# A constant tile of 41 words instead of 1, and one of 41 instead of 17, in a fused attention and SoLU kernel

## The chip, the cores and the metric

The kernel runs on one core of a Trainium2 chip. What counts is the time of one execution on the device in microseconds; shown is the median of three runs. One further execution was recorded by the hardware profiler, and every row below is from that one.

## What is computed

Sliding-window attention with a few "sink" keys (4 batches, 8 heads, 768 positions, head size 64) is followed, token by token, by two dense layers with a SoLU and a layer norm between them:

```python
scores = scale * np.matmul(q, k.transpose(0, 1, 3, 2))
keep = is_sink | in_window          # n_sink = 4, window = 128
a = softmax(np.where(keep, scores, -1e9))
x = np.matmul(a, v)                 # 3072 tokens x 512
h = x @ w_in                        # 512 -> 1024
solu = h * softmax(h)
ln = (solu - mu) / np.sqrt(var + 1e-06) * g_ln
out = ln @ w_out                    # 1024 -> 512
```

The weights arrive as 64-bit floats.

## The kernel before

**Tiles of work.** The 3072 tokens are cut into 24 blocks of 128. A block goes through scores, softmax, product with the values, the first layer (`hidden`, line 748), the SoLU, and the second layer (`project`, line 839). The order in which all these steps are issued, for all blocks together, is a table of numbers (`ORDER`) written into the kernel; each engine does its instructions in that order, and all loads and stores are issued on the queue of SyncE (SP).

**The two layers on TensorE.** Both use 4-byte words of the type float32r and give float32 accuracy by splitting: a matrix is the sum of a high and a low part, and a product is three matmuls, high x high, high x low and low x high. In `hidden` the stationary operand (the one that a weight load puts into the array) is a 128x128 slice of `xh` or `xl`, and the moving operand is 512 columns of `w1h` or `w1l`. There are 4 slices, 2 halves of the 1024 outputs and 3 products, so 24 matmuls for a block and 576 in all:

```python
for m, (a, w) in enumerate(((xh, w1h), (xh, w1l), (xl, w1h))):
    nc.tensor.matmul(st["h", n][:, cols], a[:, kt, :], w[:, kt, cols], ...)
```

`project` has the same form with `uh`, `ul` (stationary) and `w2h`, `w2l` (moving, 512 columns): 8 slices of 3 products, 24 matmuls for a block. Only the last block does its 512 columns as two halves of 256, so there are 552 matmuls of 512 columns and 48 of 256. Each matmul has its own weight load of 128 columns, which the engine makes while the matmul before it is still streaming.

**Weights.** 16 blocks of raw weights (`wraw`, 512 KB each, 4096 bytes in each of 128 partitions) are loaded by `fetch_w` (line 374) near the start. ScalarE and VectorE take them apart into `w1h`, `w1l` (in the pool `consts`) and `w2h`, `w2l` (in `wpool`, in the very buffers that `wraw` has given back).

**Where tiles lie.** Within a partition the pools lie one behind the other, and each tile is given its length rounded up to a multiple of 32 bytes. So the length of an early tile sets the place of all that is allocated behind it. `consts` holds `val`, `w1h`, `w1l`, `ok`, `allok` and, as its last tile, `general`, one word that says whether the inputs need the other, general path of the kernel. `wpool` follows, then `cpool` with the identity matrices `ident` and `ident_r`, masks, and `neg_half` (a word that holds -0.5), then `keys`, and then `sb` with `xh`, `xl`, `uh`, `ul` and all that passes through a block. In the built program the places are (bytes, and what is left modulo 256):

| tile | before | mod 256 | after | mod 256 |
|---|---|---|---|---|
| w1h, w1l (moving, layer 1) | 16544, 32928 | 160 | the same | 160 |
| w2h, w2l (moving, layer 2), wraw | 49408 + 4096 i | 0 | 49568 + 4096 i | 160 |
| ident, ident_r | 82176, 82688 | 0 | 82336, 82848 | 160 |
| keys | 85536 | 32 | 85792 | 32 |
| uh (stationary, layer 2) | 106912 + 2048 i | 160 | 107168 + 2048 i | 160 |
| xl (stationary, layer 1) | 121504 + 2048 i | 160 | 121760 + 2048 i | 160 |
| ul (stationary, layer 2) | 150176 + 2048 i | 160 | 150432 + 2048 i | 160 |
| xh (stationary, layer 1) | 181408 + 2048 i | 160 | 181664 + 2048 i | 160 |

The slices that single matmuls take begin at multiples of 512 bytes (stationary) and 2048 bytes (moving) within these, or 1024 in the halves of the last block, which leaves the remainder by 256 as it is.

Of the kernel before, what the change touches and what calls it, by code (L numbers as in the profile page):

```python
# [9 lines left out]
F32 = mybir.dt.float32  # L10
F32R = mybir.dt.float32r
I32 = mybir.dt.int32
# [111 lines left out]
P = 128  # L124
# [13 lines left out]
def kernel(  # L138
# [23 lines left out]
    with ExitStack() as fast:  # L162
        general = _banded(fast, tc, q, k, v, n_sink, window, w_in, w_out, g_ln, out, val, wts, wpool, consts)
# [7 lines left out]
def _outside(nc, consts, n_f, w_f):  # L171

    ok = consts.tile([P, 4], F32, name="ok")
    nc.vector.tensor_scalar(ok[:, 0:1], n_f, 0.0, None, op0=ALU.is_ge)
    nc.vector.tensor_scalar(ok[:, 1:2], n_f, float(NSK), None, op0=ALU.is_le)
    nc.vector.tensor_scalar(ok[:, 2:3], w_f, 1.0, None, op0=ALU.is_ge)
    nc.vector.tensor_scalar(ok[:, 3:4], w_f, float(P), None, op0=ALU.is_le)
    allok = consts.tile([P, 1], F32, name="allok")
    nc.vector.tensor_reduce(allok, ok, axis=AX.X, op=ALU.min)
    general = consts.tile([P, 1], I32, name="general")  # L180
    nc.vector.tensor_scalar(general, allok, -1.0, 1.0, op0=ALU.mult, op1=ALU.add)
    return general


def _banded(ctx, tc, q, k, v, n_sink, window, w_in, w_out, g_ln, out, val, wts, wpool, consts):
# [13 lines left out]
    cpool = ctx.enter_context(tc.tile_pool(name="cpool", bufs=1))  # L199
# [28 lines left out]
    def outside(_, j):  # L228
        st["general"] = _outside(nc, consts, n_f, w_f)
# [120 lines left out]
        for i in range(2):  # L350
            nc.vector.tensor_scalar(of_lows[:, i, :], by_head, lows[:, i:i + 1], None, op0=ALU.mult)

    neg_half = cpool.tile([P, 17], F32, name="neg_half")[:, 0:1]
    nc.vector.memset(neg_half, -0.5)


# [707 lines left out]
```

## Time and profile before

| | |
|---|---|
| median of 3 runs | 407.3 us (406.33 to 408.24) |
| the profiled execution | 407.82 us, its span 406.1 us |
| TensorE (PE) busy | 389.2 us, 96% of the span |
| VectorE, ScalarE, GpSimd busy | 301.4, 254.0, 158.2 us |
| moved by DMA | 76.24 MB, 188 GB/s on the mean |

The span is that of the core's instructions; the 1.7 us between it and the execution's own time lie outside them. A matmul's record runs past the start of the next one, since matmuls are pipelined: its duration says little of what it costs, and what counts is the distance from one start to the next.

### The profile page before, as it was taken

To read this page: it belongs to the slowest core of one execution; us is meant where nothing else is said; L and a number is where in the kernel's file an instruction comes from. 1 tells how busy PE (TensorE), PEld (TensorE's weight loads), DVE (VectorE), ACT (ScalarE), POOL (GpSimd) and SP (SyncE) were. 2 spreads that over 40 slices of the span, in tenths; PEclk is the share of its full clock that TensorE was granted. 3 is DMA by queue.
4 is the path that set the end of the run, shared out by engine and by line. 5 is a ranking of instruction groups with operands and counts; after the bars stand their busy time and mean duration, and the time that the engine had idled before them with its cause. 6 is when DMAs were issued, how large, how long until landed. Compare 5 with 4: busy or idle time off the path is not lost.

```text
span 406.1 us, 10168 instructions
## 1 busy us (share of the span) xinstructions
PE 389.2 (96%) x3667; PEld 309.4 (76%) x3667; DVE 301.4 (74%) x883; ACT 254.0 (63%) x698; POOL 158.2 (39%) x312
## 2 busy tenths in 40 slices
PE   3798999999999999999999999999999999999996
PEld 2465768877877878787778888878888788878885
DVE  3989999999999999789979687783763745542340
ACT  3999999857677687656637746655454553342451
POOL 6713171615756463713533341562520552400100
PEclk9999999999999999999999999999999999999999
DMA  7999569999998878999886667959275635503011
GB/s 208 339 301 255 137 141 209 180 222 240 240 231 232 249 214 220 268 210 277 206 224 172 161 212 149 246 167 257 103 196 149 185 126 156 178 4 106 26 53 59
DMA packets 86573, 76.24 MB, mean 188 GB/s; under 512 B 45868, under 2 KB 75444, under 8 KB 86516
## 3 DMA queue, kind: packets, MB, share of 16 engines
q1 hardware_dynamic: 86516, 75.52, 71.8%
q8 instruction: 31, 0.51, 0.5%
q14 instruction: 26, 0.21, 0.2%
HBM read 48.76 MB, written 26.87 MB: 186 GB/s over the span
## 4 chain that ended last, share of the span: by engine, by line
PE 71%; DMA 10%; DVE 7%; ACT 5%; POOL 3%; issue 2%; SPq 2%; POOLq 0%; ACTq 0%; DVEq 0%
PE o L839 28%; PE h L748 26%; PE av L728 8%; PE banks L567 5%; ACT sc L606 2%; DMA ub<-ud 2%; DMA kn<-in_k_dram 1%; DMA qn<-in_q_dram 1%; DVE sc L597 1%; DMA wraw<-in_moe_w_in_dram 1%; DMA ud<-u 1%; DMA vn<-in_v_dram 1%; PE av L718 1%; DMA pb<-pd 1%; PE banks L665 1%
## 5 line engine op out<-in xcount | busy, mean ns | idle before, releaser
L606 ACT ACTIVATE sc<-sc,nmx 128x132 f32<-128x132 f32 x192 | 75.6, 398 | 15.2 <-DVE nmx L597 15.2
L839 PE MATMUL o<-w2h,uh 128*128 128x512 f32 (+1 forms) x200 | 78.6, 393 | 0.0
L748 PE MATMUL h<-w1h,xh 128*128 128x512 f32 x192 | 77.5, 404 | 0.4 <-DVE u L763 0.4
L839 PE MATMUL o<-w2h,ul 128*128 128x512 f32 (+1 forms) x200 | 77.5, 388 | 0.0
L839 PE MATMUL o<-w2l,uh 128*128 128x512 f32 (+1 forms) x200 | 77.2, 386 | 0.0
L748 PE MATMUL h<-w1l,xh 128*128 128x512 f32 x192 | 75.3, 392 | 0.0
L748 PE MATMUL h<-w1h,xl 128*128 128x512 f32 x192 | 75.2, 392 | 0.0
L626 POOL TENSOR_TENSOR pn<-sc,rs 128x512 f32<-128x512 f32 x38 | 39.2, 1045 | 42.6 <-DMA pb<-pd 17.5
L758 ACT ACTIVATE e<-h,nm 128x1024 f32<-128x1024 f32 x24 | 26.8, 1117 | 39.3 <-DVE nm L753 37.1
L679 POOL TENSOR_SCALAR_AFFINE_SELECT pc<-pt 128x512 f32<-128x512 f32 x40 | 28.1, 711 | 57.0 <-DVE pt L656 38.9
L597 DVE CUSTOM_DVE_ANT_0 sc<-banks,bias 128x132 f32<-128x132 f32 x192 | 46.8, 286 | 2.4 <-PE banks L567 0.7
L748 PEld LDWEIGHTS h<-w1h,xh 128*128 128x128 f32 x192 | 36.0, 188 | 11.6 <-issue 2.3
L839 PEld LDWEIGHTS o<-w2h,uh 128*128 128x128 f32 x200 | 37.6, 188 | 9.6 <-issue 1.5
L839 PEld LDWEIGHTS o<-w2h,ul 128*128 128x128 f32 x200 | 37.6, 188 | 8.4
L839 PEld LDWEIGHTS o<-w2l,uh 128*128 128x128 f32 x200 | 37.6, 188 | 7.8
L753 DVE TENSOR_REDUCE nm<-h 128x1 f32<-128x1024 f32 x24 | 29.2, 1218 | 18.8 <-PE h L748 18.6
L748 PEld LDWEIGHTS h<-w1h,xl 128*128 128x128 f32 x192 | 36.0, 188 | 8.4 <-DVE xl L737 0.5
L825 DVE TENSOR_TENSOR ul<-ur,uh 128x512 fp32r<-128x512 f32 x40 | 29.1, 739 | 16.6 <-ACT uh L821 15.9
L748 PEld LDWEIGHTS h<-w1l,xh 128*128 128x128 f32 x192 | 36.1, 188 | 6.8
L567 PE MATMUL banks<-keys,q 32*64 32x200 f32 (+3 forms) x1280 | 36.8, 331 | 2.6 <-ACT keys L548 1.5
L606 ACT ACTIVATION_READ_ACCUMULATOR sc<-sc,nmx 128x1 f32 x192 | 36.8, 192 | 0.0
L567 PEld LDWEIGHTS banks<-keys,q 32*64 32x64 f32 (+1 forms) x1280 | 27.7, 133 | 10.3 <-issue 5.2
(142 smaller groups left out, 702.3 us busy)
## 6 DMA issues: line engine op xcount, KB each, us to landing
ud<-u SPq DMA_DIRECT2D x20, 512.0 KB, 3.3
ub<-ud SPq DMA_DIRECT2D x80, 128.0 KB, 3.8
pb<-pd SPq DMA_DIRECT2D x76, 128.0 KB, 3.8
vn<-in_v_dram SPq DMA_DIRECT2D x24, 256.0 KB, 5.1
out_dram<-ob SPq DMA_DIRECT2D x23, 256.0 KB, 3.3
kn<-in_k_dram SPq DMA_DIRECT2D x12, 384.0 KB, 5.8
qn<-in_q_dram SPq DMA_DIRECT2D x12, 384.0 KB, 8.7
pd<-pn SPq DMA_DIRECT2D x34, 128.0 KB, 3.7
```

Source lines behind the costliest of these rows:

```text
L567: nc.tensor.matmul(st["s", n, g][ROWS[y], x, 256 * j + at:256 * j + at + wide], st["q", n][rows, m, ROWS[y]], kk[rows, m].rearrange("p b x ...
L597: nc.vector.tensor_tensor_reduce(out=st["sc", n][:, h], in0=st["s", n, g][:, x, 256 * j + BLK:256 * j + BLK + SEG], in1=bias0 if c == 0 el ...
L606: nc.scalar.activation(sc[:, h], sc[:, h], AF.Exp, bias=nmx[:, h:h + 1], scale=-1.0, accum_out=ssum[:, h:h + 1])
L626: nc.gpsimd.tensor_tensor(st["pn", n][:, 2 * i:2 * i + 2].rearrange("p b h x -> p h b x"), st["sc", n][:, :, PARTS[i]].rearrange("p h (b x ...
L665: nc.tensor.matmul(t[ROWS[i ^ 1 if old and y == 0 else i], y, h], st["pn", n][ROWS[y], h, ROWS[i]], ident[ROWS[y], ROWS[y]], start=True, s ...
L679: nc.gpsimd.affine_select(st["pc", n][:, hs], st["pt", n][:, hs], pattern=[[0, HB], [1, P]], compare_op=ALU.is_ge, fill=0.0, base=0, chann ...
L728: nc.tensor.matmul(acc[ROWS[x], r, :], vals[:, 2 * r + x, :], p[:, 2 * r + x, :], start=alone, stop=alone or (r, i) == (NPAIR - 1, 1))
L748: nc.tensor.matmul(st["h", n][:, cols], a[:, kt, :], w[:, kt, cols], start=(kt == 0 and m == 0), stop=(kt == KT1 - 1 and m == 2))
L753: nc.vector.tensor_reduce(nm, st["h", n], axis=AX.X, op=ALU.max, negate=True)
L758: nc.scalar.activation(e, st["h", n], AF.Exp, bias=st["nm", n], scale=1.0, accum_out=se)
L825: nc.vector.tensor_tensor(ul, turned_u(n, g4), st["uh", n, g4].bitcast(F32), op=ALU.subtract)
L839: nc.tensor.matmul(st["o", n, i], a[:, kt % 4, :], part(w, kt)[:, i * wide:(i + 1) * wide], start=(kt == 0 and m == 0), stop=(kt == KT2 - ...
```

## The change

`general` becomes the first column of a tile of 41 words instead of a tile of 1: its room goes from 32 to 192 bytes. `neg_half` becomes the first column of 41 words instead of 17: its room goes from 96 to 192 bytes. What lies between the two moves up by 160 bytes, what lies behind both by 256. No instruction is added, removed or put elsewhere: on all five engines the rows of the two programs are the same, in the same order, and differ in addresses alone.

```diff
@@ -177,7 +177,7 @@
     nc.vector.tensor_reduce(allok, ok, axis=AX.X, op=ALU.min)
-    general = consts.tile([P, 1], I32, name="general")
+    general = consts.tile([P, 41], I32, name="general")[:, 0:1]
     nc.vector.tensor_scalar(general, allok, -1.0, 1.0, op0=ALU.mult, op1=ALU.add)
     return general
@@ -350,7 +350,7 @@
-    neg_half = cpool.tile([P, 17], F32, name="neg_half")[:, 0:1]
+    neg_half = cpool.tile([P, 41], F32, name="neg_half")[:, 0:1]
     nc.vector.memset(neg_half, -0.5)
```

## Rows read from the trace of the kernel before

**Rows 1.** The page: busy time, share of the span and instructions of TensorE.

```profile
PE 389.2 (96%) x3667; PEld 309.4 (76%) x3667; DVE 301.4 (74%) x883; ACT 254.0 (63%) x698; POOL 158.2 (39%) x312
```

**Rows 2.** The page: the chain that ended last, by engine.

```profile
PE 71%; DMA 10%; DVE 7%; ACT 5%; POOL 3%; issue 2%; SPq 2%; POOLq 0%; ACTq 0%; DVEq 0%
```

**Rows 3.** Waits of TensorE: total, times, longest, the two largest.

```profile
PE spread L266 <- DVE lows L347: 5.3, 1, 5.3
PE banks L567 <- ACT early_keys L548: 1.7, 1, 1.7
```

**Rows 4.** Timeline of TensorE, 274 to 277 us: start, duration, line.

```profile
274.33 0.39 PE L748 MATMUL h<-w1l,xh 128*128 128x512 f32 x1
...
275.24 0.39 PE L748 MATMUL h<-w1h,xl 128*128 128x512 f32 x1
...
275.92 0.39 PE L748 MATMUL h<-w1h,xl 128*128 128x512 f32 x1
276.15 0.40 PE L839 MATMUL o<-w2h,uh 128*128 128x512 f32 x1
```

**Rows 5.** The same timeline, 277.8 to 279.7 us.

```profile
277.79 0.39 PE L839 MATMUL o<-w2l,uh 128*128 128x512 f32 x1
...
279.66 0.39 PE L839 MATMUL o<-w2h,uh 128*128 128x512 f32 x1
```

**Rows 6.** The chain in order of time, 262 to 326 us: start, us, what.

```profile
270.77 5.54 PE h L748 x24
276.31 5.61 PE o L839 x24
281.92 4.80 PE h L748 x21
...
312.30 4.91 PE o L839 x21
```

**Rows 7.** Stretches, line 839 alone: length, PE busy (count), clock, DMA.

```profile
60.00:120.00 60.00, 11.88 (x48) 8.82 (x48) 1.00 1.01 220
120.00:228.00 108.00, 35.67 (x144) 26.73 (x144) 1.00 0.86 219
228.00:260.00 32.00, 11.67 (x48) 8.94 (x48) 1.00 0.80 200
260.00:406.10 146.10, 83.66 (x360) 63.80 (x360) 1.00 0.45 131
```

**Rows 8.** The chain in order of time, 225 to 262 us.

```profile
225.68 2.95 PE h L748 x12
...
228.70 0.56 SPq L486
...
259.58 2.51 PE av L728 x41
```

**Rows 9.** Stretches, line 748 alone.

```profile
120.00:228.00 108.00, 44.46 (x178) 32.83 (x179) 1.00 0.86 219
...
260.00:406.10 146.10, 47.74 (x192) 35.66 (x192) 1.00 0.45 131
```

**Rows 10.** Timeline of TensorE, last block: matmuls of 256 columns.

```profile
396.19 0.28 PE L839 MATMUL o<-w2h,uh 128*128 128x256 f32 x1
...
396.90 0.28 PE L839 MATMUL o<-w2h,uh 128*128 128x256 f32 x1
```

**Rows 11.** DMA issues: count, KB each, median us to landing.

```profile
ud<-u SPq DMA_DIRECT2D x20, 512.0 KB, 3.3
...
wraw<-in_moe_w_in_dram SPq DMA_DIRECT2D x8, 512.0 KB, 5.5
wraw<-in_moe_w_out_dram SPq DMA_DIRECT2D x8, 512.0 KB, 5.7
```

**Rows 12.** Stretch 10 to 20 us: PE, PEld, DVE, ACT, POOL busy, clock, DMA share, GB/s.

```profile
10.00:20.00 10.00, 6.99 (x71) 5.10 (x63) 9.27 (x42) 9.07 (x31) 7.41 (x19) 1.00 1.08 337
```

**Rows 13.** Groups of TensorE: busy us, mean ns, idle before.

```profile
L814 PE MATMUL banks<-ident,ud 128*128 128x128 f32 x32 | 4.4, 274 | 0.0
```

## The prediction

> **What bounds the kernel now.** I read the page first for the engine that is never idle. It is TensorE, busy for 96% of the span [rows 1], and 71% of the chain that ended last is its work [rows 2]. Then its waits, to see whether it is held up by anyone: the longest is 5.3 us at the very start, the next 1.7 us [rows 3]. So from about 60 us on TensorE is fed without a break, and the time is the sum of the distances between its matmuls. All stretches that I cite have a granted clock of 1.00, the level of 2.4 GHz [rows 7, 9, 12], so the clock explains no difference between them.
>
> The last view is the one that this change is about: the distance from one matmul's start to the next, in the two layers, which do the same thing (128x128 stationary, 512 moving columns, float32r, a new weight load for each). In layer 1 the starts go from 274.33 to 275.92 us in 7 steps (5 matmuls between the rows are left out, beside the one shown), 1.59 / 7 = 227 ns [rows 4]. In layer 2, some 3 us later, they go from 277.79 to 279.66 us in 8 steps, 1.87 / 8 = 234 ns [rows 5]. The chain says the same of whole runs: 24 of layer 2 take 5.61 us (234 ns each) and 21 take 4.91 (234); 24 of layer 1 take 5.54 (231) and 21 take 4.80 (229), where each run of layer 1 begins with a few slower ones before it settles at 227 [rows 6]. I find the same two levels up to the end of the trace. At its settled pace, then, a matmul of layer 2 costs 234 - 227 = 7 ns (6.6 before rounding: 233.75 - 227.1) more than the same matmul of layer 1.
>
> **What the change does to them.** What can differ between equal matmuls is where their operands lie. In layer 1 the moving and the stationary operands both begin at 160 modulo 256; in layer 2 the moving begin at 0 and the stationary at 160. The start of the slow pace is also where the place changes: up to 276.15 us the words that move are `w1`, from there on `w2`, and the weight load for the first `uh` still went on under the last `w1` matmul, which kept its 227 ns [rows 4]. After the change layer 2 stands as layer 1 does, both operands at 160, and I expect it to take layer 1's pace. The rest of the program is the same rows on every engine.
>
> - *Layer 2, 512 columns.* Its 552 such matmuls lie as follows: 48 from 60 to 120 us, 144 from 120 to 228, 48 from 228 to 260, and 360 behind that, less the 48 of 256 columns, 312 [rows 7]. I count 144 + 312 = 456. The 48 of 228 to 260 us I leave out: in that stretch a chain that begins with layer 1 on TensorE at 225.68 goes through SyncE's queue and loads and comes back to TensorE at 259.58 [rows 8], so that what TensorE saves inside it turns into a wait at its end. The chain hangs on TensorE's own work at its start, so what was saved before 228 us is kept. The 48 before 120 us I leave out for the same reason (TensorE is not on the chain in most of that time). 456 x 6.6 ns = 3.0 us.
> - *Layer 2, the 48 of 256 columns.* From 396.19 to 396.90 us 6 steps take 0.71 us, 118 ns each [rows 10]. No row shows such a matmul with operands that agree. Bounds: nothing, or the same 6.6 ns each, 0.3 us. I take nothing, since 118 is close to half of 234 but no farther above half of 227 than the reading allows.
> - *Layer 1.* Its places modulo 256 stay. Where its runs follow layer 2 directly, the slower matmuls at their start should go: a run of 21 at 4.80 us holds 4.80 - 21 x 0.2271 = 0.03 us of that [rows 6], with one such change for each of the 24 blocks a gain of 0.7 us at the most. On the other side runs that settle only after a few matmuls keep layer 2 from its full gain, by about as much. I set the one against the other.
> - *The raw weights.* `wraw` moves with `w2`, so 16 loads of 512 KB now land at 160 instead of 0. They take 5.5 to 5.7 us to landing; the stores of `u`, which leave SBUF from places at 160 and are as large, take 3.3 [rows 11], and no load here lands 4096-byte rows at 160. So nothing for sure; I take nothing, being nearest to that store, which bears its start at 160 without harm. Upper bound: 8.4 MB at the 337 GB/s of the second 10 us are 25 us of transfers [rows 12]; if each row of 4096 bytes cost one more piece of 256, that is 1/16 or 1.6 us, and all of it on the path only if nothing else covered it. VectorE and ScalarE, busy 9.3 and 9.1 of those 10 us [rows 12], cover most of it.
> - *Identity matrices, masks.* They are read by short transposes and mask operations, whose pace no pair of rows compares. The transposes of `u` by `ident`, at both ends of the run, are 32 [rows 13]; at 6.6 ns either way that is 0.2 us. I take nothing.
>
> The Trainium skill, in "DMA: Bandwidth & Descriptors", section "How a descriptor splits into AXI transactions", says that a transaction must start at a multiple of 256 B, so that a descriptor which doesn't is cut into one more. By that the loads of `wraw` would each have 17 transactions for 16, and the kernel could lose up to the 1.6 us above; no run here shows it so far.
>
> **The sum.** 407.82 us of the profiled execution less 3.0 is 404.8. That execution was 0.5 us above the median of the runs (407.3), so for the median I forecast 407.3 - 3.0 = 404.3 us, or 0.74% less. A difference under 0.5% (2.0 us) is about what a measurement of this kernel can't tell from none.
>
> **The rivals.**
> *No change.* Where the operands lie may have nothing to do with the 7 ns; the layers also write to different PSUM tiles, and take their stationary operand from different producers. Then the time stays 407.3. For it speaks only that a difference between two groups is not an experiment; against it that both paces are so steady, and that neither DMA nor another engine changes at 276.15 us. The Trainium skill is on its side: "SBUF — State Buffer", section "Who interferes with whom", gives TensorE two independent read ports, one for the moving operand and one for weight loads, and says that only the port pair of VectorE and GpSimd contends; by that rule the two operands can't hinder each other wherever they lie. The trace at least has some cause that this rule doesn't name, since 227 and 234 ns stand side by side.
> *Slower: the true period is 512 bytes.* The stationary tiles of both layers move by 256, `w1` doesn't. Modulo 512 `w1` lies at 160, and `xh`, `xl` lie at 160 before and at 416 after, so layer 1 would lose the agreement that it has, and fall to 234 ns. That costs 370 matmuls of layer 1 in the two stretches that count [rows 9] 6.6 ns each, 2.4 us, with more before 120 us. Layer 2 would agree only in its products with `ul` (both at 416), a third of 456: 1.0 us back at best, nothing if one disagreeing product spoils the next. The time is 408.7 to 409.7. Against it: the last `w1` matmul before 276.15 us runs while a `uh` slice at 416 modulo 512 is loaded (it lies at 111008), and the 4 steps from 275.24 to 276.15 take 0.91 us, 227.5 ns each [rows 4]. It decides if agreement is judged modulo 512 or more in most matmuls, not in one at a boundary.
> *Faster, but not by as much.* If the chain of 228 to 260 us [rows 8] or loads elsewhere don't move up with TensorE, the 144 matmuls before it give nothing: 312 x 6.6 = 2.1 us, 405.2. With half of the bound on `wraw` as well, 406.
>
> **How the numbers follow.** The forecast's case, layer 2 at layer 1's pace and most of it kept, 403.5 to 405.2: 60%. Faster by less than that (405.2 to 406.5): 13%. No effect: 17%. Slower by the period of 512 bytes, or by `wraw` without the gain: 7%. More than forecast (all 552 and the 48 short ones, and layer 1's starts, 4.6 us in all): 3%. The range is to leave out the slower case and part of "no effect" on its upper side, with the runs' own spread, and reaches to 407.5; below, to 402.8 for the largest gain. The likeliest case alone has 403.0 to 405.2. Of the 13% half are under 0.5%. So faster 0.69, same 0.23, slower 0.08.
>
> **What would show it.** Right: the distance of starts at line 839 is 227 ns in settled runs, as at line 748 before, and stays there across the change of layer; line 748 stays at 227; the page has the same instructions, and TensorE's waits stay small but for some tenths near 100 and 260 us. Wrong: line 839 stays at 234 (places don't matter); line 748 goes to 234 (period 512); line 839 is faster, but TensorE waits more, and the waits name DMA, SyncE or GpSimd; or `wraw` lands later than 5.5 us and the first 60 us grow.

## The result and the profile after

The changed kernel takes 404.51 us (median of seven runs) against 407.31 us of the kernel before. One of the seven took 974.09 us and is left out of the ratio; the other six took 402.86 to 404.88. The ratio is 0.9915, 95% interval 0.9895 to 0.9935, so it is 0.85% faster, 3.5 us by the ratio, where 3.0 were forecast. The page of the kernel after, its first line and the chain by engine:

```profile
PE 384.6 (96%) x3667; PEld 308.6 (77%) x3667; DVE 301.2 (75%) x883; ACT 254.1 (63%) x698; POOL 158.6 (39%) x312
PE 82%; DMA 5%; DVE 5%; ACT 3%; issue 2%; SPq 2%; POOL 1%; DVEq 0%; ACTq 0%; POOLq 0%
```

The instructions are the same in number, TensorE is busy for the same share of the span [rows 1], and more of the chain is its own [rows 2]. The timeline of TensorE after, at the change from layer 1 to layer 2 that rows 4 and 5 show (start, duration, line):

```profile
271.38 0.39 PE L748 MATMUL h<-w1l,xh 128*128 128x512 f32 x1
...
273.65 0.39 PE L748 MATMUL h<-w1h,xl 128*128 128x512 f32 x1
273.87 0.39 PE L839 MATMUL o<-w2h,uh 128*128 128x512 f32 x1
274.10 0.39 PE L839 MATMUL o<-w2l,uh 128*128 128x512 f32 x1
...
276.37 0.39 PE L839 MATMUL o<-w2h,ul 128*128 128x512 f32 x1
```

Ten steps of layer 1 (271.38 to 273.65) take 2.27 us, 227 ns each, as before [rows 4]. Ten steps of layer 2 (274.10 to 276.37) take 2.27 us as well, 227 ns each, where they took 234 [rows 5]; the pace doesn't change where the layer changes. The chain of the kernel after, in order of time, with the pieces that answer to rows 6 and 8 (start, us, what):

```profile
224.21 2.95 PE h L748 x12
...
256.40 3.65 PE av L728 x64
260.05 5.66 PE o L839 x24
...
268.48 5.55 PE h L748 x24
274.04 5.44 PE o L839 x24
279.48 4.76 PE h L748 x21
```

A run of 24 of layer 2 went from 5.61 to 5.44 us (226.7 ns each). The run of 21 of layer 1 behind it went from 4.80 to 4.76 [rows 6]: it doesn't begin with slower matmuls any more. TensorE's waits, the two longest, are 5.0 and 1.9 us, both in the first 60 us (compare [rows 3]):

```profile
PE spread L266 <- DVE lows L347: 5.0, 1, 5.0
PE banks L514 <- DVE nmx L597: 1.9, 1, 1.9
```

### The profile page after: what moved, and what is told of

Its sections match the earlier page's. It is cut to its first block, busy times and chain, and to the rows that moved or that the text cites. A ratio compares the mean times of both kernels' runs of the same rounds, so it can differ in the third digit from the quotient of the medians.

```text
span 401.6 us, 10168 instructions
## 1 busy us (share of the span) xinstructions
PE 384.6 (96%) x3667; PEld 308.6 (77%) x3667; DVE 301.2 (75%) x883; ACT 254.1 (63%) x698; POOL 158.6 (39%) x312
## 4 chain that ended last, share of the span: by engine, by line
PE 82%; DMA 5%; DVE 5%; ACT 3%; issue 2%; SPq 2%; POOL 1%; DVEq 0%; ACTq 0%; POOLq 0%
PE o L839 31%; PE h L748 29%; PE av L728 9%; PE banks L567 6%; DMA wraw<-in_moe_w_in_dram 2%; DMA kn<-in_k_dram 2%; DMA pb<-pd 2%; PE ws L408 2%; ACT sc L606 1%; PE banks L665 1%; PE av L718 1%; DVE sc L597 1%; PE banks L814 1%; DVE keys L540 1%; PE banks L514 1%
## 5 line engine op out<-in xcount | busy, mean ns | idle before, releaser
L839 PE MATMUL o<-w2h,uh 128*128 128x512 f32 (+1 forms) x200 | 77.7, 389 | 0.0
L839 PE MATMUL o<-w2h,ul 128*128 128x512 f32 (+1 forms) x200 | 76.3, 381 | 0.0
L839 PE MATMUL o<-w2l,uh 128*128 128x512 f32 (+1 forms) x200 | 76.2, 381 | 0.0
L825 DVE TENSOR_TENSOR ul<-ur,uh 128x512 fp32r<-128x512 f32 x40 | 28.1, 715 | 16.9 <-ACT uh L821 16.9
L763 DVE SCALAR_TENSOR_TENSOR u<-h,e 128x1024 f32<-128x1024 f32 x24 | 29.2, 1219 | 8.8 <-ACT e L758 8.5
```

Of the source, the lines that this page charges most:

```text
L763: nc.vector.scalar_tensor_tensor(u, st["h", n], -1.0 / DFF, st["e", n], op0=ALU.mult, op1=ALU.mult, accum_out=nmu)
L825: nc.vector.tensor_tensor(ul, turned_u(n, g4), st["uh", n, g4].bitcast(F32), op=ALU.subtract)
L839: nc.tensor.matmul(st["o", n, i], a[:, kt % 4, :], part(w, kt)[:, i * wide:(i + 1) * wide], start=(kt == 0 and m == 0), stop=(kt == KT2 - ...
```

## The experiments

The main theory, called A below, is that the moving words and the stationary words of a matmul must begin at the same place modulo 256 bytes. All ten kernels issue the same instructions in the same order as the kernel before, and differ in where tiles begin. The distance d is the place of the moving words less that of the stationary ones, modulo 256: before, 0 in layer 1 and 96 in layer 2. In each kernel the same three pieces of the chain near 270 us are read, a run of 24 of layer 1, one of 24 of layer 2 and one of 21 of layer 1, since nothing but the matmuls themselves bounds them.

**The two edits apart, and all at another place.** Three kernels, timed six to twelve times each.

The first keeps only `general` (d = 96 in both layers):

```diff
-    general = consts.tile([P, 1], I32, name="general")
+    general = consts.tile([P, 41], I32, name="general")[:, 0:1]
```

Expected: 

> Only the longer tile of general: w1 stays at 160, w2 moves to 160, and the stationary tiles of both layers to 64 modulo 256. Theory A (moving and stationary words must begin at the same place modulo 256): both layers disagree now, settled distances of 234 ns at line 839 and at line 748; layer 1 loses 2.5 to 3.5 us, so the ratio to the kernel before is 1.005 to 1.010. Theory B (only the place of the moving words counts, 160 is good, 0 is bad): 227 ns in both layers, ratio 0.990 to 0.994, as with the whole change. Theory C (places do nothing, the gain was something else in the program's layout): line 748 at 227, line 839 at 234, ratio 0.997 to 1.003.

Ratio 1.0049, interval 1.0032 to 1.0065 (409.13 us). The chain of this kernel:

```profile
271.97 5.67 PE h L748 x24
277.64 5.60 PE o L839 x24
283.24 4.90 PE h L748 x21
```

Now layer 1 is slow too: 4.90 us for 21, 233 ns each, and layer 2 stays so (5.60 us for 24, 233 ns). One half of the change alone makes the kernel slower, with `w2` at the very place that it has in the whole change. That rules out theory B (160 is a good place for moving words) and theory C. The loss, 2.0 us by the ratio, is smaller than the 2.5 to 3.5 that were expected, and the ratio just under the expected 1.005 to 1.010. Layer 1's runs were not all settled at 227 before: the run of 21 lost 4.90 - 4.80 us [rows 6], 5 ns for each matmul and not 7.

The second keeps only `neg_half` (d = 160 in layer 1, 0 in layer 2):

```diff
-    neg_half = cpool.tile([P, 17], F32, name="neg_half")[:, 0:1]
+    neg_half = cpool.tile([P, 41], F32, name="neg_half")[:, 0:1]
```

Expected: 

> Only the longer tile of neg_half: w1 stays at 160, w2 stays at 0, the stationary tiles of both layers move to 0 modulo 256. Theory A (agreement modulo 256): the layers change roles, 227 ns at line 839 and 234 at line 748; the gain of one is the loss of the other, ratio 0.997 to 1.003. Theory B (the moving words' place alone): as before, 234 at line 839 and 227 at line 748, and the same ratio, so the two lines tell them apart and the time doesn't.

Ratio 0.9984, interval 0.9970 to 0.9998. The chain of this kernel:

```profile
270.58 5.68 PE h L748 x24
276.26 5.46 PE o L839 x24
281.72 4.91 PE h L748 x21
```

The layers have changed roles: layer 2, untouched at 0, now takes 5.46 us for 24 (227.5 ns), since its stationary words have come to 0; layer 1 takes 4.91 for 21 (234 ns). The time alone, 0.16% less, would have said next to nothing.

The third is the whole change and, ahead of `w1`, a tile that is 96 bytes longer (d = 0 in both layers):

```diff
-    val = consts.tile([P, 2], F32, name="val")
+    val = consts.tile([P, 32], F32, name="val")[:, 0:2]
```

Expected: 

> The whole change and a longer first tile (val, 32 words), so that w1, w2 and the stationary tiles of both layers all begin at 0 modulo 256. Theory A (agreement, wherever it lies): 227 ns in both layers, ratio 0.989 to 0.994 as with the whole change. Theory B (moving words at 0 are slow): 234 ns in both layers, ratio 1.005 to 1.010. If the loads of raw weights gain from landing at 0, the first 60 us are shorter than with the whole change by up to 1.6 us, and the ratio is below 0.989.

Ratio 0.9924, interval 0.9904 to 0.9944, no different from the whole change. The chain of this kernel:

```profile
267.59 5.55 PE h L748 x24
273.14 5.44 PE o L839 x24
278.58 4.76 PE h L748 x21
```

The same three numbers as in the changed kernel, with all operands at 0 instead of 160. So it is the agreement that counts, and not the place. The ratio is not below 0.989 either, so the raw weights, which land at 0 here, show no gain from it.

**Other distances.** Three kernels, one run each, which give each layer a distance of its own:

```diff
-    general = consts.tile([P, 1], I32, name="general")
+    general = consts.tile([P, 17], I32, name="general")[:, 0:1]
...
-    neg_half = cpool.tile([P, 17], F32, name="neg_half")[:, 0:1]
+    neg_half = cpool.tile([P, 33], F32, name="neg_half")[:, 0:1]
```

and the same with 49 and 57 words for `neg_half`. Expected of them, in this order: 

> Longer tiles of general (17 words) and neg_half (33): the moving words begin 128 bytes behind the stationary ones in layer 1 and 32 in layer 2 (modulo 256). If agreement modulo 128 is enough, line 748 keeps 227 ns; if it must be modulo 256, both lines stand at 234. If the cost grows with the distance instead, the two lines differ, with line 839 nearer to 227.

> General 17 words, neg_half 49: the moving words begin 64 bytes behind the stationary ones in layer 1 and 224 (32 ahead of them) in layer 2. If agreement modulo 64 is enough, line 748 keeps 227 ns; if modulo 256, both lines stand at 234 ns, ratio near 1.005.

> General 17 words, neg_half 57: the moving words begin 32 bytes behind the stationary ones in layer 1 and 192 in layer 2. With agreement modulo 256 both lines stand at 234 ns. If some distance other than 0 is better than agreement, a line is under 227 ns in one of these three kernels.

The chains: first d = 128 in layer 1 and 32 in layer 2,

```profile
276.39 5.60 PE o L839 x24
281.99 4.88 PE h L748 x21
```

then 64 and 224,

```profile
275.93 5.59 PE o L839 x24
281.52 4.81 PE h L748 x21
```

then 32 and 192:

```profile
277.15 5.60 PE o L839 x24
282.75 4.90 PE h L748 x21
```

None is at 227 ns. With d = 64 one row more is needed, since 4.81 us for 21 is no more than the kernel before took with d = 0 (4.80 [rows 6], where the run begins with slower matmuls). The next run of 24 of layer 1 in the kernel with 64 and 224 is

```profile
292.62 5.60 PE h L748 x24
```

That is 233 ns each. The same run in the kernel before, and then in the changed one, took 228 and 227 ns each:

```profile
293.03 5.48 PE h L748 x24
```

```profile
290.36 5.44 PE h L748 x24
```

So with d = 64 the same line has two paces in one execution, 229 ns in some runs and 233 in others, and neither is 227. The single times, 408.21, 407.43 and 408.83 us beside 406.80 of the kernel before, say no more than that none is faster. Two more kernels, one run each, go below 32 bytes, by words cut off at the start of longer tiles (4 words here, 1 in the other; the tiles grow by 256 bytes, so all else keeps its place):

```diff
-    wts = [consts.tile([P, DM // P, DFF], F32R, name=nm) for nm in ("w1h", "w1l")] + ...
+    wts = [consts.tile([P, DM // P * DFF + 64], F32R, name=nm)[:, 4:4 + DM // P * DFF]
+           .rearrange("p (k f) -> p k f", f=DFF) for nm in ("w1h", "w1l")] + ...
```

Expected: 

> The whole change, with w1h and w1l cut 16 bytes into longer tiles: the moving words of layer 1 begin 16 bytes behind the stationary ones (176 against 160 modulo 256), layer 2 agrees at 160. If agreement must hold to less than 16 bytes, line 748 stands at 230 to 234 ns; if it need only hold to within 16 bytes or more, 227. Line 839 at 227 either way.

> As the run with 16 bytes, with 4: the moving words of layer 1 begin one word behind the stationary ones. If a common group of 16 bytes or more is what counts, line 748 keeps 227 ns; if the cost needs exact agreement, 230 to 234. If being a little late is better than agreement, under 227.

The chains, with 16 bytes and then with 4:

```profile
275.03 5.46 PE o L839 x24
280.50 4.87 PE h L748 x21
```

```profile
276.28 5.45 PE o L839 x24
281.73 4.96 PE h L748 x21
```

Their single times are 405.48 and 407.22 us. In these two nothing but `w1` has moved against the changed kernel (modulo 256), and layer 1 alone has lost its pace. All distances together, from the run of 21 (layer 1) or 24 (layer 2), us divided by the count; d = 0 is the changed kernel:

| d, bytes | 0 | 4 | 16 | 32 | 64 | 96 | 128 | 160 | 192 | 224 |
|---|---|---|---|---|---|---|---|---|---|---|
| layer 1, ns | 227 | 236 | 232 | 233 | 229 | 233 | 232 | 234 | | |
| layer 2, ns | 227 | | | 233 | | 233 | | | 233 | 233 |

Agreement is the best of the ten distances, and agreement modulo 4, 16, 32, 64 or 128 will not do instead. What was expected of d = 32 against 96 (a cost that grows with the distance) didn't show: the cost is 2 to 10 ns and follows no order in d. 64 is the mildest, though only in some of its runs (above), and a single word the worst, worse than any of the tile-sized distances.

**Which two must agree.** In a product of three matmuls the operand loaded under a matmul is not always the one that it multiplies by: `xl` is loaded under `w1l` x `xh` and used with `w1h`. The whole change with unused tiles around `xl`:

```diff
+        sb.tile([P, 40], F32, tag="ahead", name="ahead", bufs=1)
         st["minus"] = sb.tile([P, P], F32, tag="xl", name="minus", bufs=2)
+        sb.tile([P, 24], F32, tag="behind", name="behind", bufs=1)
```

Expected: 

> The whole change and unused tiles of 160 and 96 bytes ahead of and behind the buffers of xl: xl alone begins at 64, all other operands of both layers at 160 modulo 256. Layer 2 keeps 227 ns. In layer 1, if moving words hinder the weight load that runs under them (the next stationary operand), the step that begins with the product of w1l and xh is slow, since xl is loaded under it; if they hinder their own stationary operand, the step of w1h and xl. Either way about a third of the loss of a whole disagreement: 227 + 7/3, that is 229 to 230 ns on the mean in layer 1's settled runs, and 1 us more time than the whole change. If a single disagreement spoils all three, 234.

The chain of this kernel, whose lines stand two lower (750 for 748, 841 for 839):

```profile
271.64 5.67 PE h L750 x24
277.31 5.48 PE o L841 x24
282.79 4.90 PE h L750 x21
```

One run took 407.70 us beside 406.80 of the kernel before. Layer 2 keeps its pace, and layer 1 is as slow as if everything disagreed, 233 ns: not a third of the loss but all of it. The last of the three cases in the expectation holds, and neither of the first two. In the timeline of this kernel no one step bears the loss: from the tenth matmul of a run on, the distance from `w1h` x `xh` to the next start is 233 ns on the mean, from `w1l` x `xh` 235 and from `w1h` x `xl` 232. A last kernel puts `w1l` at 64 too, so that each moving operand agrees with what is loaded under it:

```diff
-    wts = [consts.tile([P, DM // P, DFF], F32R, name=nm) for nm in ("w1h", "w1l")] + ...
+    wts = [consts.tile([P, DM // P * DFF + more], F32R, name=nm)[:, 0:DM // P * DFF]
+           .rearrange("p (k f) -> p k f", f=DFF) for nm, more in (("w1h", 40), ("w1l", 24))] + ...
```

Expected: 

> On top of the run with xl alone at 64: w1l begins at 64 too, w1h and xh stay at 160, layer 2 agrees. Now each moving operand agrees with the stationary operand that is loaded under it (w1h with xh, w1l with xl, w1h with xh), but two of three disagree with the stationary operand that they are multiplied by. Theory L (what must agree is the moving operand and the weight load under it): 227 ns at layer 1's line (750 here), a ratio of 0.989 to 0.994 as with the whole change. Theory O (the moving operand and its own stationary operand), or a rule that all four must agree: 233 to 234 ns there, a ratio of 0.998 to 1.002.

Ratio 0.9977, interval 0.9965 to 0.9990 (ten runs). The chain:

```profile
270.61 5.63 PE h L750 x24
276.24 5.44 PE o L841 x24
281.68 4.86 PE h L750 x21
```

4.86 / 21 = 231 ns: better than with `xl` alone apart, but not 227. So agreement with the load under the matmul is not enough. That the matmul's own stationary operand is what must agree is not shown by it either: this kernel has more such disagreements than the one before it, two of three against one of three, and is faster. What the runs show is that a layer runs at 227 ns when all four of its operands agree; which pair does what in between, and by what mechanism, stays open.

## Why the prediction was right, step by step

- *What bounds the kernel.* Held. With TensorE hardly waiting after the first 60 us, what its matmuls saved came out of the time, and what they lost in the first experiment was added to it.
- *The cause of the 7 ns.* The step from "two groups differ" to "their places are the cause" rested on one comparison of two layers. The experiments carry it: the two edits apart, by which a layer goes slow or fast as its own operands disagree or agree, and the third kernel, which moves all of them together without effect.
- *The sum.* 3.0 us was forecast, 3.5 measured. How the gain adds up can be read by setting the start of the same matmul in both traces side by side, at four places: the first of layer 2 near 122 us, the 12 of layer 1 at 225.68 [rows 8] (224.21 after), the first of layer 2 behind `av` near 262 us (260.05 after), and the first of 256 columns at 396.19 [rows 10]. The rows that are not shown yet, of the kernel before

```profile
122.01 5.79 PE o L839 x24
...
262.20 5.79 PE o L839 x24
```

  and of the kernel after

```profile
121.33 5.69 PE o L839 x24
...
391.78 0.28 PE L839 MATMUL o<-w2h,uh 128*128 128x256 f32 x1
```

  | stretch, by the kernel before | forecast, us | gained, us |
  |---|---|---|
  | up to 122.01 | 0 | 0.7 |
  | 122.01 to 225.68 | 1.0 | 0.8 |
  | 225.68 to 262.20 | 0 | 0.7 |
  | 262.20 to 396.19 | 2.1 | 2.3 |

  These two executions lie 4.5 us apart (407.82 and 403.29 us), further than the ratio of all runs says. In the two stretches that were counted the forecast holds: layer 2's distances gave 2.6 us there, less than 6.6 ns for each matmul, because runs of layer 2 that do not follow layer 1 still begin with slower ones (5.66 us for 24 at 260.05, against 5.44), and layer 1's gave 0.5. Those were the two that had been set against each other.
- *The stretch left out.* This step was wrong: from 225.68 to 262.20 us TensorE was to lose at the end what it saved inside, since a chain through SyncE led out of it and back. At its end that chain hung on one short pause. Before, the matmul of `av` that waits for GpSimd starts 0.37 us after the one ahead of it, as shown by the rows of four around it, which otherwise follow each other in 0.22 us:

```profile
259.10 0.39 PE L728 MATMUL av<-pc,vn 128*64 128x128 f32 x4
259.58 0.44 PE L728 MATMUL av<-pt,vn 128*64 128x128 f32 x4
```

  In the other eleven traces, the slower kernel with `general` alone among them, the same matmul follows in 0.10 us. After the change the chain stays on TensorE there, and 0.7 us was gained: 0.3 from the 48 matmuls of layer 2, 0.3 from that pause, which owes nothing to layer 2's pace. The 48 before 120 us, left out for the same reason, gave 0.2 as well. The other 0.5 of the first stretch was there at 30 us, before any of layer 2; at that place the three kernels of the first experiments are between 0.2 us behind and 1.3 ahead of the kernel before, so it is not a gain that can be told from one execution.
- *256 columns.* Right to take nothing. After, they stand 120 ns apart (last section), and so they did before on the mean of all 48; the 118 of [rows 10] was a short stretch of an uneven pattern.
- *The raw weights.* Right to take nothing. The loads after:

```profile
wraw<-in_moe_w_in_dram SPq DMA_DIRECT2D x8, 512.0 KB, 5.6
wraw<-in_moe_w_out_dram SPq DMA_DIRECT2D x8, 512.0 KB, 6.7
```

  The second row is 1.0 us above that of before [rows 11], but with `neg_half` alone, where the raw weights land at 0 as before, the same rows are

```profile
wraw<-in_moe_w_in_dram SPq DMA_DIRECT2D x8, 512.0 KB, 5.6
wraw<-in_moe_w_out_dram SPq DMA_DIRECT2D x8, 512.0 KB, 7.1
```

  so that the place doesn't decide it. By the rule of the Trainium skill that was cited ("DMA: Bandwidth & Descriptors", "How a descriptor splits into AXI transactions") these loads would have a transaction more when they land at 160. The section speaks of where a read starts, and whether a place of landing counts in the same way no run here shows; the runs show no time for it.
- *The rivals.* "No change" is out, by the interval and by the experiments, which leave the PSUM tiles and the producers of both layers as they were. By the rule of the Trainium skill that spoke for it ("SBUF — State Buffer", "Who interferes with whom": two independent read ports) the two read streams of TensorE can't hinder each other. The measurement decides against the forecast that was drawn from it here, since the pace changes by 2 to 10 ns with nothing but addresses; whether it is these two streams that meet is not shown. The period of 512 bytes is out as well: after the change `w1` lies at 160 and `xh` and `xl` at 416 modulo 512, and layer 1 keeps 227 ns. Modulo 128 isn't enough either (d = 128: 232 ns).

## What to carry to other kernels

In a kernel bound by a dense stream of matmuls, put the distance of starts of like matmuls side by side before anything else: a steady difference of 3% between two layers that issue the same instructions is worth an explanation. If their operands begin at different places modulo 256 bytes, a few unused words in a constant tile ahead of them are a cheap edit to try. The runs show the effect for float32r matmuls of 128x128 by 512 columns, each with its own weight load, and for nothing else. Any edit that changes the length of an early tile moves all that lies behind it, so a small gain or loss of such an edit may come from places alone, as that of the first experiment here does.

## What was not expected

One operand apart from three others costs a layer as much as full disagreement (233 ns, the run with `xl` apart). A start that is off by a single word is the worst distance of all (236 ns). With d = 64 the same line changes between two paces in one execution. And matmuls of 256 columns have another best distance than those of 512. In the timeline of the last block, the kernel after (d = 0) has 9 steps from 393.09 to 394.17, 120 ns each,

```profile
393.09 0.28 PE L839 MATMUL o<-w2h,ul 128*128 128x256 f32 x1
...
394.17 0.28 PE L839 MATMUL o<-w2h,ul 128*128 128x256 f32 x1
```

and the kernel with d = 192 in layer 2 has 15 steps from 398.10 to 399.80, 113 ns each:

```profile
398.10 0.28 PE L839 MATMUL o<-w2h,ul 128*128 128x256 f32 x1
...
399.80 0.28 PE L839 MATMUL o<-w2h,ul 128*128 128x256 f32 x1
```

With 48 of them that is 0.3 us against some 3 us of the others; no kernel here beats the changed one beyond its interval.
